# Radix-4 sums of four tiles as TensorE products, and a PSUM bank moved from the general ring to the first layer of the FFN, in a planned attention, FFT and FFN kernel

## The chip, the cores and the metric

The kernel runs on one core of one Trainium2 chip. The metric is the device time of one execution in microseconds; lower is better.

## The reference

Inputs: q, k, v of shape (8 batches, 8 heads, 576 positions, 64), float32, and the two weight matrices `w_ch1` (512 x 2048) and `w_ch2` (2048 x 512), which arrive as 8-byte floats. Output: (8, 576, 512), float32.

```python
scores = (1 / sqrt(64)) * q @ k.T            # causal window of 64 positions, else -1e9
attn   = softmax(scores) ; x = attn @ v      # x: (8, 576, 512), the heads side by side
mixed  = real(fft(fft(x, axis=1), axis=2))   # over the positions, then over the 512 columns
u      = x + mixed
un     = (u - mean(u)) / sqrt(var(u) + 1e-6) # over the 512 columns
out    = u + relu(un @ w_ch1) @ w_ch2
```

## The kernel before, in words

The 4608 rows are cut into 36 tiles T of 128 rows; nine tiles make a pair of batches. Each kind of work is written as a list of operations given to a planner (`Plan`), and nothing runs in the order in which it is written.

**Stages.** `attn_tile(T)` computes one tile of attention. Tiles 0 to 12 (`whole`) work in float32 with TensorE transposes; each fills nine PSUM banks: `pk` and `pq` (keys and queries turned), `psc` twice (scores), `pp` twice (probabilities turned), `pa` twice (attention times values), `py` (below). Tiles 13 to 35 split float32 into two float16 parts and turn them by DMA. In either form `normed` divides by the softmax's sum on VectorE (DVE), `radix4` makes four sums and differences of the 128-column quarters of x (two adds or subtracts of 128x256, two of 128x128, on DVE or GpSimd/POOL), and `flip_y` turns the four results onto the other axis by four TensorE transposes into a bank `py` (or by DMA in most tiles from 13 on). `fft(b)` does the two transforms of one batch when its tiles are there (after T = 4 and T = 8 of a pair), `norm_tile(T)` adds x and normalises, `ffn(c)` is the two-layer FFN of a chunk c of two tiles. For chunk 0 the FFN is in float32; for the other 17 each float32 product is three float16 products. The weights are converted from 8-byte floats by three DVE operations a piece (32 pieces, `conv`), and after chunk 0's use split into float16 parts (`weight_split`).

**FFN loop.** For each of 16 blocks f of 128 hidden columns `bank1`/`one` (line 1197) makes `ph` by 12 matmuls, ACT (line 1212) and DVE (line 1215) empty it into two float16 parts `hh`, and `second` (line 1178) multiplies these into `po`. Two blocks f share a bank of the ring `f1`; the bank is free when DVE's line 1215 of the second block is done.

**Rings.** Eight PSUM banks: `ps` 4 (all attention, FFT and normalisation stages but the first FFT's `pg`), `f1` 2, `f2` 2 (FFN output).

**The planner.** Each operation has an engine (or two, with `alt` and a margin), a duration, a latency, a priority (smaller is sooner) and the buffers it reads and writes. `order()` simulates the engines greedily from these durations and writes out one instruction order for each engine; the semaphores then hold that order on the chip, and every engine works its own queue strictly in order. All DMAs but the indirect ones are issued from SyncE's one queue (SP). Where the planned TensorE gap is over 0.8 us and no FFN has run yet, dummy matmuls (`warm`, line 1276) are written into it. `slack` is an allowance: an operation that can run on TensorE counts its inputs as ready later by `slack * LATE` of the engine that made them (DVE and ACT 0.5 us, POOL 0.7, DMA 1.0). It is 0.5 for tiles from T = 9 on and 0 for the first nine and for the FFN. A bank that comes free gets no such allowance.

```python
        "ps": 4, "f1": 2, "f2": 2,
                late = x.slack * self.LATE[o.eng] if "PE" in x.durs else 0.0
        op("POOL", 2.35, base + 7, radix4, [bx], [by], alt=("DVE", 1.2, LAZY_Y if T < 4 else lazy))
                nc.tensor.transpose(t["py"][:, j], t["y"][:, j], ident)
```

Of the kernel before, what the change touches and what calls it, by code (L numbers as in the profile page):

```python
# [12 lines left out]
F32 = mybir.dt.float32  # L13
# [28 lines left out]
Y_SOON = (4, 8)  # L42
LAZY, LAZY_FFT, LAZY_U = 0.4, 0.4, 0.5
LAZY_E, LAZY_Y = 0.3, 0.8
WARM = 0.8, 0.4
EARLY, LATER = 80, -20
PRO = 13
PITCH, FFT_AT, NORM_AT, FFT1 = 8.5, 13, 6, 0
SLACK = 0.5
PLAIN = 1  # L50
W_DMA, W_DMA_STEP, W_CONV, W_SQ, W_SPLIT, W_STEP = -40, 1.0, 20, 60, 60, 0.3
VS = 64.0
# [73 lines left out]
class Op:  # L126
    __slots__ = ("eng", "dur", "lat", "fn", "deps", "outs", "prio", "wait", "ready", "allocs", "bufs", "idx", "durs", "margin", "port", "slack")


class Plan:  # L130
# [13 lines left out]
    def __init__(self, rings, fifo):  # L144
        self.rings, self.fifo, self.ops, self.gaps = dict(rings), fifo, [], []
        self.slack = 0.0

    def op(self, eng, dur, prio, fn, reads=(), writes=(), lat=0.0, alt=(), holds=(), port=True):
# [4 lines left out]
        o.durs = {e: d + self.FIXED[e] for e, d in ([(eng, dur), alt[:2]] if alt else [(eng, dur)])}  # L153
        o.port, o.slack = port, self.slack
        o.margin = alt[2] if len(alt) > 2 else self.MARGIN
# [40 lines left out]
    def order(self):  # L196
# [23 lines left out]
        while len(res) < n:  # L220
# [77 lines left out]
def attn_fft_ffn_kernel(ctx: ExitStack, tc: tile.TileContext, q, k, v, w1, w2, gidx, dft_d, dft_s, mask, out):  # L298
# [112 lines left out]
    def attn_tile(T, base):  # L411
# [17 lines left out]
        bk, bq, bv = Buf("kq"), Buf("kq"), Bfl[3]  # L429
        op("DMA", 1.45, base - 8, lambda: load("kn", "kq", k), writes=[bk], lat=2.0)  # L430
        op("DMA", 1.45, base - 8, lambda: load("qn", "kq", q), writes=[bq], lat=2.0)
        if whole:
            op("DMA", 1.45, base - 6, lambda: load("vw", None, v), writes=[Bva[i]], lat=2.0)
        else:
            op("DMA", 1.45, base - 6, lambda: load("vn", None, v), writes=[bv], lat=2.0)

# [38 lines left out]
        else:  # L475
# [26 lines left out]
            op("POOL", 1.12, base + 0.1, k_lo, [bk], [bkp], alt=("DVE", 0.6, lazy))  # L502
            op("DMA", TURN, base + 0.2, k_turn, [bkp], [bkT], lat=2.0)
            op("ACT", 0.95, base + 0.5, lambda e: q_part(0, e), [bq], Bfl[4:6], alt=("DVE", 0.6, lazy))
            op("POOL", 2.1, base + 0.6, lambda e: q_part(1, e), [bq], Bfl[4:6], alt=("DVE", 1.13, lazy))
            for j in range(2):
                op("DMA", TURN, base + 0.7, lambda j=j: q_turn(j), Bfl[4:6], [Bq[i]], lat=2.8)
        if T == PRO and n > 0:

            def k_tail():  # L510
                src = kst32[:, (T - 1) % 3 * 512 : (T - 1) % 3 * 512 + 512].rearrange("p (a s) -> p a s", a=4)
                dst = kst16[:, before * 1024 : before * 1024 + 1024].rearrange("p (h s) -> p h s", h=H)
                for h in range(2):
# [9 lines left out]
            op("DVE", 1.6, base + 0.3, k_tail, [BkT[(T - 1) % 3]], [BkT[before], Buf("tail")])  # L523

# [32 lines left out]
        for jj in range(2):  # L557
# [73 lines left out]
            bpt[jj] = [bt, bt2]  # L631
            op("DMA", HTURN, base + 4.2 + jj, lambda g=p_turn: g(0), [bpp], [bt, bt2], lat=1.8)
            op("DMA", HTURN, base + 4.3 + jj, lambda g=p_turn: g(1), [bpp], [bt2], lat=1.8)

# [4 lines left out]
        for hf in range(2):  # L639
# [20 lines left out]

            def normed(hf=hf):
                pa = t["pa", hf]
                xv = xts[T].rearrange("p (h d) -> p h d", h=H)
                rc = sm.tile([P, 4, 1], F32, tag="rc", name=f"rc{T}_{hf}")
# [78 lines left out]
        def flip_y():  # L743
# [23 lines left out]
        if soon:  # L767
            op("PE", 0.44, base + 8, flip_y, [by, Bid], [bpy, *first])
        else:
            byp = Buf("up")  # L770
            op("ACT", 0.52, base + 7.5, y_hi, [by], [byp], alt=("DVE", 0.34, lazy))
            op("DVE", 0.6, base + 7.6, y_lo, [by], [byp])
            op("DMA", TURN, base + 7.7, y_turn, [byp], [bpy], lat=2.2)
        for a in keeps:
            op(*a, port=not soon)

    def fft(b, base):
# [120 lines left out]
        for cl in (1, 2, 0):  # L898
# [43 lines left out]
            op("PE", 0.67 if cl == 0 else 1.32, base + 5, sstage, [*(bg[gi] for _, gi in use), Bds], [bpz, bmp])  # L942
            op("ACT", 0.65, base + 5.1, odd, [bpz], [bmp])
            op("DVE", 1.2, base + 5.2, mix, [bpz], [bmp], port=False)
            if b == 0:
# [119 lines left out]
    def weight_piece(x, g, order):  # L1065
# [49 lines left out]
        op("DVE", 0.6, pr - 0.2, lambda: conv(2), bw, [bf])  # L1115
        op("ACT", 0.72, W_SQ + W_STEP * order, square, [bf], [bj, Bssq[x]])

# [127 lines left out]
    for T in range(NTT):  # L1245
        if T == PRO:
            to_parts()
        base = PITCH * T + (LATER if T > 4 else -EARLY)
        plan.slack = SLACK if T >= NT else 0.0
        attn_tile(T, base)  # L1250
        pb, n = divmod(T, NT)
# [5 lines left out]
        if T == 4:  # L1257
# [50 lines left out]
```

## Time and profile before

| | |
|---|---|
| median of three runs | 1010.4 us (1010.17 to 1551.11) |
| profiled execution | 1014.19 us, its span 1012.4 us |
| TensorE (PE) busy | 975.3 us, 96% of the span |
| VectorE (DVE) busy | 671.6 us, 66% |
| ACT busy | 417.3 us, 41% |
| POOL busy | 205.8 us, 20% |
| FFN's first product | 93.2 us after the start |

The span is what the trace shows; the execution lasts 1.8 us longer than it. Busy times are of one engine; an engine's waits are given with the engine and line that released it, and L1197 is line 1197 of the kernel above. The dummy matmuls count as busy.

### The profile page before, as it was taken

How to read it: one execution, taken by the hardware profiler on the slowest of the kernel's cores; microseconds unless marked ns; L12 is line 12 of the kernel's file. 1: busy time of each engine (PE TensorE's matmuls, PEld its weight loads, DVE VectorE, ACT ScalarE, POOL GpSimd, SP SyncE). 2: the span in 40 equal slices, each digit the busy share in tenths (PEclk: the TensorE clock that was granted, in tenths of full speed). 3: DMA queues.
4: the chain of work that ended last, by engine and by line, in shares of the span. 5: the costliest groups of instructions: out<-in, count | busy, mean ns of one | idle time of the engine just before them, and what ended most of it. 6: DMA issues, size and time to landing. Idle time of an engine off the chain costs nothing.

```text
span 1012.4 us, 22555 instructions
## 1 busy us (share of the span) xinstructions
PE 975.3 (96%) x8793; PEld 692.1 (68%) x8793; DVE 671.6 (66%) x1972; ACT 417.3 (41%) x1044; POOL 205.8 (20%) x211
## 2 busy tenths in 40 slices
PE   8888999999998999999999999999999999999998
PEld 6776768766675666666676667666676667666664
DVE  5889898887876758676776668666786555441121
ACT  6665667563544444344452345322454223211111
POOL 1001001133224403352132203141121300310000
PEclk9988999999999999999999999999999999999999
DMA  8978766533859896988768575857564411220000
GB/s 192 232 199 232 188 193 146 103 72 75 148 124 167 168 152 137 163 151 148 152 127 169 101 137 106 160 117 149 90 128 103 83 32 45 63 63 21 1 21 22
DMA packets 310955, 123.60 MB, mean 122 GB/s; under 512 B 292728, under 2 KB 292856, under 8 KB 310848
## 3 DMA queue, kind: packets, MB, share of 16 engines
q1 hardware_dynamic: 308128, 113.24, 55.3%
q0 software_dynamic: 2720, 8.92, 3.2%
q8 instruction: 69, 1.13, 0.5%
q14 instruction: 38, 0.31, 0.1%
HBM read 54.97 MB, written 14.17 MB: 68 GB/s over the span
## 4 chain that ended last, share of the span: by engine, by line
PE 73%; DMA 10%; DVE 9%; SPq 3%; ACT 2%; issue 2%; POOL 1%; DVEq 0%; ACTq 0%; POOLq 0%
PE ph L1197 31%; PE po L1178 28%; PE pa L657 3%; PE pg L878 2%; PE pz L910 2%; PE psc L568 2%; DMA uhl<-up 2%; DMA pt<-flex 2%; PE psc L575 2%; DMA kn<-in_k 1%; DMA mt<-md,gix 1%; DVE hh L1215 1%; SPq L626 1%; DMA qn<-in_q 1%; DVE y L691 1%
## 5 line engine op out<-in xcount | busy, mean ns | idle before, releaser
L1197 PE MATMUL ph<-uhl,w0s 128*128 128x256 f16 (+1 forms) x3384 | 427.5, 277 | 9.3 <-DVE hh L1215 8.6
L1178 PE MATMUL po<-w1s,hh 128*128 128x512 f16 (+1 forms) x1696 | 426.0, 387 | 0.2
L1197 PEld LDWEIGHTS <-w0s 128*128 128x128 f16 x3264 | 318.5, 98 | 96.8 <-issue 14.3
L1215 DVE SCALAR_TENSOR_TENSOR hh<-ph,hh 128x256 f16<-128x256 f32 x272 | 114.6, 422 | 223.8 <-ACT hh L1212 212.2
L1212 ACT ACTIVATE hh<-ph 128x256 f16<-128x256 f32 x272 | 104.1, 383 | 375.5 <-PE ph L1197 264.5
L1178 PEld LDWEIGHTS <-hh 128*128 128x128 f16 x1632 | 155.9, 98 | 139.5 <-issue 1.0
L595 ACT ACTIVATE pr<-pr,nm 128x128 f32<-128x128 f32 x288 | 91.3, 393 | 16.3 <-DVE nm L587 16.3
L587 DVE CUSTOM_DVE_ANT_0 pr<-psc,mskb 128x128 f32<-128x128 f32 x288 | 65.7, 286 | 15.9 <-PE psc L568 11.8
L1012 POOL TENSOR_TENSOR rs<-mv,mhalf 128x1 f32<-128x1 f32 x36 | 21.6, 599 | 181.0 <-DVE mv L1008 160.2
L1035 POOL TENSOR_TENSOR up<-un,up 128x512 f16<-128x512 f32 x33 | 39.0, 1183 | 70.4 <-ACT up L403 63.6
L620 POOL TENSOR_TENSOR flex<-pr,flex 128x512 f16<-128x512 f32 x25 | 30.0, 1202 | 109.5 <-ACT flex L403 90.7
L657 PE MATMUL pa<-va,pt 128*64 128x65 f16 (+1 forms) x760 | 41.5, 207 | 5.7 <-DMA pt<-flex 5.1
L988 POOL DMA_INDIRECT mt<-md,gix x34 | 35.9, 1057 | 52.0 <-DMA md<-mp 46.4
L657 PE MATMUL pa<-ve,pt 128*64 128x65 f16 (+1 forms) x760 | 42.0, 208 | 0.1
L484 POOL TENSOR_TENSOR flex<-kn,flex 128x512 f16<-128x512 f32 x19 | 22.7, 1197 | 83.6 <-ACT flex L403 82.1
L403 ACT CAST flex<-pr 128x512 f16<-128x512 f32 x38 | 23.5, 620 | 27.7 <-DMA pt<-flex 25.5
L669 DVE TENSOR_TENSOR xu<-pa,rc 128x256 f32<-128x256 f32 x72 | 30.6, 425 | 2.9 <-DMA out<-xu 0.3
L568 PE MATMUL psc<-kst,qbd 128*128 128x128 f32 x208 | 29.8, 293 | 2.5 <-ACT qbd L403 1.2
L691 DVE TENSOR_TENSOR y<-xu 128x256 f32<-128x256 f32 x70 | 30.2, 472 | 0.6
L657 PEld LDWEIGHTS <-pt 128*64 128x64 f16 x1104 | 20.8, 112 | 14.0 <-issue 7.2
L568 PEld LDWEIGHTS psc<-kst,qbd 128*128 128x128 f32 x208 | 26.9, 203 | 4.5 <-issue 1.9
L910 PE MATMUL pz<-g,ds__75 97*96 97x257 f16 (+3 forms) x240 | 29.2, 273 | 0.5 <-DVE g L888 0.5
(156 smaller groups left out, 1115.1 us busy)
## 6 DMA issues: line engine op xcount, KB each, us to landing
wd<-in_moe_w_ch SPq DMA_DIRECT2D x20, 512.0 KB
out<-xu SPq DMA_DIRECT2D x36, 256.0 KB
ve<-va SPq DMA_DIRECT2D x67, 130.0 KB
kn<-in_k SPq DMA_DIRECT2D x32, 256.0 KB
qn<-in_q SPq DMA_DIRECT2D x32, 256.0 KB
flex<-in_moe_w_ch SPq DMA_DIRECT2D x12, 512.0 KB
flex<-in_v SPq DMA_DIRECT2D x20, 256.0 KB
md<-mp SPq DMA_DIRECT2D x24, 192.0 KB
```

The source lines that it names most:

```text
L568: nc.tensor.matmul(p_[:, hp], qw, keys(hp, jj), start=True, stop=True)
L587: nc.vector.tensor_tensor_reduce(out=t["pr", jj][:, hp], in0=t["ps", jj][:, hp], in1=mskb[:, m : m + P], scale=-0.125, scalar=3.0e38, op0= ...
L595: nc.scalar.activation(pr, pr, AF.Exp, bias=t["nm", jj][:, hp : hp + 1], scale=-1.0)
L657: nc.tensor.matmul(pa[64 * jj : 64 * jj + 64, hh], pt[:, sl], v_, start=(x == 0), stop=(x == len(mm) - 1))
L691: eng.tensor_tensor(out=o, in0=p0, in1=p1, op=al)
L910: nc.tensor.matmul(pz[:M, c0:c1], ds_[:NJ, a, c[0] : c[0] + c[1]], t["g", gi][:, b_, c0:c1], start=(x == 0), stop=(x == len(mm) - 1),)
L988: nc.gpsimd.indirect_dma_start(out=mts[T], out_offset=None, in_=mds[pb][0 : HR if n < 4 else 2 * HR], in_offset=bass.IndirectOffsetOnAxis( ...
L1035: eng.tensor_tensor(out=t["up"][:, 1], in0=t["un"], in1=t["up"][:, 0], op=ALU.subtract)
L1178: nc.tensor.matmul(t["po"][i], l_, r_, start=(f == 0 and x == 0), stop=(f == NKF - 1 and x == len(mm) - 1))
L1197: nc.tensor.matmul(ph, l_, r_, start=(x == 0), stop=(x == len(mm) - 1))
L1212: nc.scalar.activation(t["hh", f][:, 0], ph, AF.Relu)
L1215: nc.vector.scalar_tensor_tensor(out=hh[:, 1], in0=ph, scalar=0.0, in1=hh[:, 0], op0=ALU.max, op1=ALU.subtract)
```

## The change

1. For T in `Y_SUMS` = (1, 2, 3, 4) the operation `radix4` is gone. `flip_y` reads x itself and makes each of the four turned sums by accumulating float32 matmuls of the quarters against the identity or its negative (`minus`, a new constant made on POOL): 4 + 4 + 2 + 2 = 12 matmuls in place of 4 transposes.
2. The ring `ps` has 3 banks in place of 4, `f1` 3 in place of 2.
3. `normed` is cut in two: the reciprocal stays on DVE, and the multiplication may go to ACT as four scaled copies of 128x64.
4. The planner gets a second allowance, `wary`: operations that cannot run on TensorE count inputs from another engine as late by 0.6 `LATE` in all stages but the conversion of the weights and the FFN of chunks 1 to 17; `slack` for TensorE becomes 0.
5. Planned durations and DMA latencies are set anew, and so are priorities (tiles from T = 5 on 30 us later, weight conversion 20, squares 50, split 10 later, the weights' DMAs 10 later, the second FFT of the first pair 10 later, since it has 20 less of its own) and margins for the choice of engine.

```diff
-LAZY, LAZY_FFT, LAZY_U = 0.4, 0.4, 0.5
+LAZY, LAZY_FFT, LAZY_U = 0.1, 0.8, 0.2
-EARLY, LATER = 80, -20
+EARLY, LATER = 80, 10
-PITCH, FFT_AT, NORM_AT, FFT1 = 8.5, 13, 6, 0
-SLACK = 0.5
+PITCH, FFT_AT, NORM_AT, FFT1 = 8.5, 13, 9, -20
+SLACK = 0.0
+SLACK_V = 0.6
+WARY = 0
+LAZY_N = 0.0
+Y_SUMS = (1, 2, 3, 4)
-W_DMA, W_DMA_STEP, W_CONV, W_SQ, W_SPLIT, W_STEP = -40, 1.0, 20, 60, 60, 0.3
+W_DMA, W_DMA_STEP, W_CONV, W_SQ, W_SPLIT, W_STEP = -30, 1.0, 40, 110, 70, 0.3
...
-                late = x.slack * self.LATE[o.eng] if "PE" in x.durs else 0.0
+                late = self.LATE[o.eng] * (x.slack if "PE" in x.durs else 0.0 if o.eng in x.durs else x.wary)
...
-        "ps": 4, "f1": 2, "f2": 2,
+        "ps": 3, "f1": 3, "f2": 2,
...
-            op("DMA", HTURN, base + 4.2 + jj, lambda g=p_turn: g(0), [bpp], [bt, bt2], lat=1.8)
+            op("DMA", HTURN, base + 4.2 + jj, lambda g=p_turn: g(0), [bpp], [bt, bt2], lat=2.4)
...
+            def normed(eng, hf=hf):
+                pa, rc = t["pa", hf], t["rc", hf]
+                xv = xts[T].rearrange("p (h d) -> p h d", h=H)[:, 4 * hf : 4 * hf + 4]
+                if eng is nc.scalar:
+                    for hh in range(4):
+                        nc.scalar.mul(xv[:, hh], pa[:, hh, 0:64], rc[:, hh])
+                else:
+                    eng.tensor_tensor(out=xv, in0=pa[:, :, 0:64], in1=rc.to_broadcast([P, 4, 64]), op=ALU.mult)
...
-            op("DVE", 0.75, base + 6.2 + 0.5 * hf, normed, [bpa], [bx], port=False)
+            brc = Buf()
+            op("DVE", 0.26, base + 6.2 + 0.5 * hf, recip, [bpa], [brc], port=False)
+            op("DVE", 0.32, base + 6.25 + 0.5 * hf, normed, [bpa, brc], [bx], alt=("ACT", 0.95, LAZY_N), port=False)
...
-        op("POOL", 2.35, base + 7, radix4, [bx], [by], alt=("DVE", 1.2, LAZY_Y if T < 4 else lazy))
+        summed = T in Y_SUMS
+        if not summed:
+            op("POOL", 3.2, base + 7, radix4, [bx], [by], alt=("DVE", 1.2, LAZY_Y if T < 4 else lazy))
...
-            for j in range(4):
-                nc.tensor.transpose(t["py"][:, j], t["y"][:, j], ident)
+            for j, terms in enumerate(((0, 1, 2, 3), (0, 5, 2, 7), (0, 6), (1, 7))):
+                if summed:
+                    for x, m in enumerate(terms):
+                        quarter = xts[T][:, P * (m % 4) : P * (m % 4) + P]
+                        nc.tensor.matmul(
+                            t["py"][:, j], quarter, ident if m < 4 else minus, start=(x == 0), stop=(x == len(terms) - 1)
+                        )
+                else:
+                    nc.tensor.transpose(t["py"][:, j], t["y"][:, j], ident)
...
-            op("PE", 0.44, base + 8, flip_y, [by, Bid], [bpy, *first])
+            op("PE", 2.85 if summed else 0.44, base + 8, flip_y, [bx if summed else by, Bid], [bpy, *first])
...
+        plan.wary = SLACK_V if T >= WARY else 0.0
```

Of the other latencies, loads of q, k and v go from 2.0 to 2.5 us, the turning of keys from 2.0 to 2.2, of queries from 2.8 to 3.0, of y from 2.2 to 3.0; `radix4` on POOL is planned at 3.2 us for 2.35.

## Rows read from the trace of the kernel before

**Rows 1.** The page's first two parts: busy time of each engine, and PE's busy share in 40 equal slices of the span, 25.3 us each (tenths).

```profile
PE 975.3 (96%) x8793; PEld 692.1 (68%) x8793; DVE 671.6 (66%) x1972; ACT 417.3 (41%) x1044; POOL 205.8 (20%) x211
PE   8888999999998999999999999999999999999998
```

**Rows 2.** Busy time of each engine in seven stretches of the span (columns: stretch, its length, then each engine's busy us with its instructions, granted clock, DMA share, GB/s).

```profile
0.00:16.00 16.00, 12.63 (x110) 10.34 (x111) 5.35 (x31) 7.93 (x18) 3.33 (x13) 1.00 0.87 178
16.00:47.50 31.50, 27.63 (x292) 23.37 (x290) 27.05 (x118) 22.73 (x60) 1.87 (x1) 0.95 0.92 223
47.50:72.00 24.50, 20.41 (x199) 17.99 (x199) 21.61 (x54) 14.27 (x38) 0.69 (x2) 0.86 0.82 211
72.00:93.20 21.20, 15.40 (x149) 12.86 (x147) 19.43 (x61) 12.81 (x34) 2.82 (x3) 0.84 0.82 232
93.20:200.00 106.80, 106.80 (x749) 79.81 (x748) 94.76 (x270) 68.16 (x167) 12.79 (x13) 1.00 0.67 163
200.00:810.00 610.00, 594.69 (x5852) 413.09 (x5850) 434.61 (x1288) 255.19 (x634) 168.97 (x164) 1.00 0.69 130
810.00:1012.40 202.40, 197.75 (x1454) 134.69 (x1452) 68.78 (x157) 36.21 (x95) 15.34 (x16) 1.00 0.13 34
```

**Rows 3.** The same stretches for the dummy matmuls of line 1276 alone (PE busy, PEld busy, clock, DMA share, GB/s): the stretch from 16 us, and the answer's sum over all seven.

```profile
16.00:47.50 31.50, 2.38 (x16) 1.57 (x16) 0.95 0.92 223
...
sum 1012.40, PE 19.45 PEld 13.83; mean PE 2.78 PEld 1.98
```

**Rows 4.** What PE waited for between 200 and 810 us (total us, times, longest).

```profile
PE ph L1197 <- DVE hh L1215: 8.0, 12, 1.7
PE pa L657 <- DMA pt<-flex: 5.1, 4, 3.2
PE py L750 <- DVE y L691: 0.9, 1, 0.9
```

**Rows 5.** The longest of PE's waits for line 1215 and another of over a microsecond: timelines of DVE and of PE (start us, us, what; in brackets the idle time before and who ended it).

```profile
545.05 0.43 DVE L407 CAST flex<-kn 128x512 f16<-128x512 f32 x1 [2.70 <-DMA kn<-in_k]
545.39 0.42 DVE L1215 SCALAR_TENSOR_TENSOR hh<-ph,hh 128x256 f16<-128x256 f32 x1
...
540.13 1.47 PE L1197 MATMUL ph<-uhl,w0s 128*128 128x256 f16 x12
541.44 1.46 PE L1178 MATMUL po<-w1s,hh 128*128 128x512 f16 x6
542.74 1.47 PE L1197 MATMUL ph<-uhl,w0s 128*128 128x256 f16 x12
545.86 2.30 PE L1197 MATMUL ph<-uhl,w0s 128*128 128x256 f16 x18 [1.65 <-DVE hh L1215]
...
685.62 0.69 DVE L1000 TENSOR_TENSOR xu<-xu,mt 128x511 f32<-128x511 f32 x1 [1.73 <-DMA mt<-md,gix]
...
687.90 1.47 PE L1197 MATMUL ph<-uhl,w0s 128*128 128x256 f16 x12 [1.39 <-DVE hh L1215]
```

**Rows 6.** What PE waited for before the FFN begins, 0 to 93.2 us (the four longest).

```profile
PE pp L606 <- ACT pr L595: 3.7, 1, 3.7
PE pk L464 <- DMA kn<-in_k: 3.1, 2, 2.5
PE pk L464 <- ACT qbd L403: 1.7, 1, 1.7
PE pq L464 <- DMA qn<-in_q: 1.5, 2, 0.9
```

**Rows 7.** From the chain that ended last, cut to 0 to 105 us (start us, us, what): float32 products of 128 columns at full and at half clock, float32 transposes, a DMA of weights, and the FFN's first product.

```profile
30.67 2.95 PE psc L568 x16
...
36.72 0.89 PE psc L568 x8
...
74.28 4.86 DMA flex<-in_moe_w_ch
...
93.21 5.18 PE ph L1197 x24
98.40 0.44 PE py L750 x4
```

**Rows 8.** DVE's timeline: the radix-4 sums of tiles 1 and 4, with what follows.

```profile
25.95 0.76 DVE L691 TENSOR_TENSOR y<-xu 128x256 f32<-128x256 f32 x2
26.63 0.61 DVE L691 TENSOR_TENSOR y<-y 128x128 f32<-128x128 f32 x2
...
46.31 0.76 DVE L691 TENSOR_TENSOR y<-xu 128x256 f32<-128x256 f32 x2
...
47.52 0.96 DVE L794 TENSOR_TENSOR yT<-yT 128x772 f32<-128x772 f32 x1
```

**Rows 9.** Groups by line over the whole span (count, busy us, mean ns): the normalising multiplication on DVE, and ACT reading PSUM in its smallest form.

```profile
L669 DVE TENSOR_TENSOR xu<-pa,rc 128x256 f32<-128x256 f32 x72 | 30.6, 425 | 2.9 <-DMA out<-xu 0.3
L927 ACT COPY mp<-pz 96x2 f32<-96x2 f32 (+1 forms) x24 | 4.1, 173 | 0.0
```

**Rows 10.** Filling and emptying of `ps` banks: the first row of PE's timeline that fills one after 16.2 us, and the DVE row that empties the last one counted (34 fillings, begun between 16.25 and 44.2 us).

```profile
16.25 0.60 PE L464 MATMUL pk<-ident,kn 128*128 128x128 f32 x4
...
45.85 0.42 DVE L669 TENSOR_TENSOR xu<-pa,rc 128x256 f32<-128x256 f32 x1
```

More of the change, by code (lines that the diff above doesn't have):

```diff
@@ L126 @@
 class Op:
-    __slots__ = ("eng", "dur", "lat", "fn", "deps", "outs", "prio", "wait", "ready", "allocs", "bufs", "idx", "durs", "margin", "port", "slack")
+    __slots__ = ("eng", "dur", "lat", "fn", "deps", "outs", "prio", "wait", "ready", "allocs", "bufs", "idx", "durs", "margin", "port", "slack", "wary")
 class Plan:
@@ L145, in __init__ @@
         self.rings, self.fifo, self.ops, self.gaps = dict(rings), fifo, [], []
-        self.slack = 0.0
+        self.slack = self.wary = 0.0
     def op(self, eng, dur, prio, fn, reads=(), writes=(), lat=0.0, alt=(), holds=(), port=True):
@@ L153, in op @@
         o.durs = {e: d + self.FIXED[e] for e, d in ([(eng, dur), alt[:2]] if alt else [(eng, dur)])}
-        o.port, o.slack = port, self.slack
+        o.port, o.slack, o.wary = port, self.slack, self.wary
         o.margin = alt[2] if len(alt) > 2 else self.MARGIN
@@ L323, in attn_fft_ffn_kernel @@
     ident = cp.tile([P, P], F32, name="ident")
+    minus = cp.tile([P, P], F32, name="minus")
     mhalf = cp.tile([P, 1], F32, name="mhalf")
@@ L362, in attn_fft_ffn_kernel @@
     op("POOL", 0.3, -500, lambda: make_identity(nc, ident), writes=[Bid])
+    op("POOL", 0.4, -480, lambda: nc.gpsimd.tensor_scalar(out=minus, in0=ident, scalar1=-1.0, scalar2=None, op0=ALU.mult), [Bid], [Bid])
     op("POOL", 0.1, -499, lambda: nc.gpsimd.memset(mhalf, -0.5), writes=[Bmh])
@@ L429, in attn_tile @@
         bk, bq, bv = Buf("kq"), Buf("kq"), Bfl[3]
-        op("DMA", 1.45, base - 8, lambda: load("kn", "kq", k), writes=[bk], lat=2.0)
-        op("DMA", 1.45, base - 8, lambda: load("qn", "kq", q), writes=[bq], lat=2.0)
+        op("DMA", 1.45, base - 8, lambda: load("kn", "kq", k), writes=[bk], lat=2.5)
+        op("DMA", 1.45, base - 8, lambda: load("qn", "kq", q), writes=[bq], lat=2.5)
         if whole:
-            op("DMA", 1.45, base - 6, lambda: load("vw", None, v), writes=[Bva[i]], lat=2.0)
+            op("DMA", 1.45, base - 6, lambda: load("vw", None, v), writes=[Bva[i]], lat=2.5)
         else:
-            op("DMA", 1.45, base - 6, lambda: load("vn", None, v), writes=[bv], lat=2.0)
+            op("DMA", 1.45, base - 6, lambda: load("vn", None, v), writes=[bv], lat=2.5)
         bkT = BkT[T % 3]
@@ L502, in attn_tile @@
             op("POOL", 1.12, base + 0.1, k_lo, [bk], [bkp], alt=("DVE", 0.6, lazy))
-            op("DMA", TURN, base + 0.2, k_turn, [bkp], [bkT], lat=2.0)
+            op("DMA", TURN, base + 0.2, k_turn, [bkp], [bkT], lat=2.2)
             op("ACT", 0.95, base + 0.5, lambda e: q_part(0, e), [bq], Bfl[4:6], alt=("DVE", 0.6, lazy))
@@ L506, in attn_tile @@
             for j in range(2):
-                op("DMA", TURN, base + 0.7, lambda j=j: q_turn(j), Bfl[4:6], [Bq[i]], lat=2.8)
+                op("DMA", TURN, base + 0.7, lambda j=j: q_turn(j), Bfl[4:6], [Bq[i]], lat=3.0)
         if T == PRO and n > 0:
@@ L521, in k_tail @@
                     nc.vector.tensor_tensor(out=lo, in0=old, in1=hi, op=ALU.subtract)
-            op("DVE", 1.6, base + 0.3, k_tail, [BkT[(T - 1) % 3]], [BkT[before], Buf("tail")])
+            op("DVE", 3.0, base + 0.3, k_tail, [BkT[(T - 1) % 3]], [BkT[before], Buf("tail")])
         def v_part(z):
@@ L631, in attn_tile @@
             bpt[jj] = [bt, bt2]
-            op("DMA", HTURN, base + 4.2 + jj, lambda g=p_turn: g(0), [bpp], [bt, bt2], lat=1.8)
-            op("DMA", HTURN, base + 4.3 + jj, lambda g=p_turn: g(1), [bpp], [bt2], lat=1.8)
+            op("DMA", HTURN, base + 4.2 + jj, lambda g=p_turn: g(0), [bpp], [bt, bt2], lat=2.4)
+            op("DMA", HTURN, base + 4.3 + jj, lambda g=p_turn: g(1), [bpp], [bt2], lat=2.4)
         bx, by = Buf("xu"), Buf("y")
@@ L659, in av, with recip @@
                             )
-            def normed(hf=hf):
+            def recip(hf=hf):
                 pa = t["pa", hf]
-                xv = xts[T].rearrange("p (h d) -> p h d", h=H)
-                rc = sm.tile([P, 4, 1], F32, tag="rc", name=f"rc{T}_{hf}")
+                rc = t["rc", hf] = sm.tile([P, 4, 1], F32, tag="rc", name=f"rc{T}_{hf}")
                 nc.vector.tensor_scalar(
@@ L772, in attn_tile @@
             op("DVE", 0.6, base + 7.6, y_lo, [by], [byp])
-            op("DMA", TURN, base + 7.7, y_turn, [byp], [bpy], lat=2.2)
+            op("DMA", TURN, base + 7.7, y_turn, [byp], [bpy], lat=3.0)
         for a in keeps:
@@ L942, in fft @@
             op("PE", 0.67 if cl == 0 else 1.32, base + 5, sstage, [*(bg[gi] for _, gi in use), Bds], [bpz, bmp])
-            op("ACT", 0.65, base + 5.1, odd, [bpz], [bmp])
-            op("DVE", 1.2, base + 5.2, mix, [bpz], [bmp], port=False)
+            op("ACT", 0.39, base + 5.1, odd, [bpz], [bmp])
+            op("DVE", 1.03, base + 5.2, mix, [bpz], [bmp], port=False)
             if b == 0:
@@ L1115, in weight_piece @@
         op("DVE", 0.6, pr - 0.2, lambda: conv(2), bw, [bf])
-        op("ACT", 0.72, W_SQ + W_STEP * order, square, [bf], [bj, Bssq[x]])
+        op("ACT", 0.53, W_SQ + W_STEP * order, square, [bf], [bj, Bssq[x]])
     def weight_scale(x, prio):
@@ L1263, in attn_fft_ffn_kernel @@
                 weight_split(x, g, W_SPLIT + W_STEP * i)
-    plan.slack = 0.0
+    plan.slack = plan.wary = 0.0
     for c in range(PLAIN, NCH):
```

3 lines of the change are left out of this document (removed).

## Prediction

> **What bounds the kernel now.** I read the busy shares first. TensorE is busy 96% of the span, VectorE 66%, and the slices show PE at nine tenths or more from the fourth on but for one [rows 1]. So a microsecond counts only where PE stands still, runs dummies or runs at half clock. The stretches say where that is [rows 2]. Before the first FFN product, at 93.2 us, PE is busy 12.63 + 27.63 + 20.41 + 15.40 = 76.1 us, of which up to 19.45 are dummies [rows 3]: some 36 of the 93.2 us are idle or dummy, and the granted clock means 0.84 to 0.95 in three of the four stretches. From 93.2 to 200 PE has no idle time. From 200 to 810 it is idle 610 - 594.69 = 15.3 us, and after that 4.7. DVE is the other full engine of the start: 27.05 of 31.50 us from 16 to 47.5, when tiles 1 to 4 are made.
>
> What ended PE's waits in the long middle is in the list of waits [rows 4]: 8.0 us in 12 waits of the first FFN layer for DVE's line 1215 (the emptying of an `f1` bank), 5.1 us in 4 waits for the DMA that turns probabilities, 0.9 for a radix-4 sum. The timelines show what the 8.0 us are [rows 5]. At 542.3 us DVE has nothing left but an instruction that waits for keys still in flight; the DMA lands at 545.05, and only behind that cast does line 1215 run, at 545.39; PE, out of banks, had been idle for 1.65 us. At 685.62 it is a gathered `mt` in place of keys. DVE isn't slow there; its order puts a DMA's landing ahead of the bank's release, and PE has one other bank to live on.
>
> **The change part by part.** The sum is made against the profiled execution (1014.2 us, 3.8 above the median of the runs shown), and its differences are put on the median.
>
> *The third `f1` bank.* A bank holds two blocks of the FFN. A block is 12 matmuls of the first layer and six of the second, which begin 1.31 and 1.30 us before the next ones [rows 5]. So one more bank lets PE work on for up to 5 us when DVE is stuck, and the longest such wait is 1.65 us [rows 5]. All of the 8.0 us [rows 4] are within reach. I take -7.5 and leave 0.5, as a planner that sees three free banks will again plan up to the third. Bounds: -8.0, and 0 if it does so everywhere (a rival below).
>
> *The third bank taken from `ps`.* No row of PE's waits from 200 us on names the emptying of a `ps` bank [rows 4]. There a tile is made every 22 us or so, and fills four of them. I charge +1, bounds 0 and +3 (the 0.9 us of the one `py` wait, three times). In the start it is otherwise: nine fillings to a tile. Pairing each filling's first write with its last read in the timelines gives 34 fillings in 28 us (the first and the last are in [rows 10]), held 1.96 us on average, 66.7 bank-us: 2.4 banks of four are taken. This goes into the next term and into a rival.
>
> *The sums as products.* Removed: four DVE instructions a tile for tiles 1 to 4, 25.95 to 27.24, so 1.3 us a tile [rows 8], 5.2 us of DVE's 27.05 in that stretch. Added: 12 float32 products for 4 transposes. Eight records of `psc`, that is four products, take 0.89 us, four transposes 0.44 [rows 7]; so 12 x 0.222 = 2.67 against 0.44, +2.23 us a tile and +8.9 us in all at full clock (at half clock, where 16 records took 2.95 us, two thirds more). Per tile the chain from x to `py` goes from 1.3 + 0.44 to 2.67 us: longer by 0.9, but without DVE's queue in the middle. Is there room on PE? In 16 to 47.5 it is busy 27.63, 2.38 of it dummies; 25.25 + 8.9 = 34.2 us for a stretch of 31.5 [rows 2, 3]. So PE, not DVE, would set this stretch, at +2.6 us. If instead DVE stays the limit, it is -5.2. If later PE work (tiles 5 and 6) is pushed behind 93.2, where PE is full, all of the 8.9 is paid. I take 0 for the start: the two limits nearly cancel, the tile-4 sum just ahead of the FFT's first fold [rows 8] is a real relief, and the 36 us of idle and dummy time can take 8.9 us of products. Bounds -5.2 and +8.9.
>
> A rule speaks against this part. The Trainium skill (Perfetto Trace Analysis, Transposes) asks that a logical transpose be done as a transpose and not as a standard matmul, and its page TensorE: Matmul & The Clock Gate (Terms) calls transpose mode four times faster for float32. The rows agree on the direction but say twice, 0.222 against 0.111 us; by the page's factor, as an estimate, the 12 products would take 5.3 us and the four tiles +19 us instead of +8.9. The rows decide.
>
> *The later allowances and latencies.* The turning of probabilities was planned to land 1.8 us after its issue plus 0.5 of slack for PE, 2.3; now 2.4, and 0.6 x 0.7 = 0.42 are allowed ahead of it where POOL made the part, so 2.8. Half a microsecond more takes 0.5 off each of the four waits of 5.1 us [rows 4]: -2.0. Bounds: -5.1, and 0. Against it, PE's own allowance goes to zero, so a late ACT or DVE is met unpadded; before 93.2 us, where it was zero already, the longest such waits are 3.7 (about when the chain runs through a weights' DMA of 4.86 us) and 1.7 us [rows 6, 7]. In the middle PE has FFN work to interleave, so +1, bounds 0 and +5. What is queued behind an unpadded wait is all of PE's order.
>
> *The split of `normed`.* On DVE nothing is added, as the same three instructions run. Where ACT takes the multiplication, DVE loses 0.425 us and ACT gets four small copies of at least 0.173 each [rows 9], 0.7 us or more; ACT is busy 22.73 of 31.5 us in the tightest stretch [rows 2]. Nothing of PE's path: 0.
>
> *The moved priorities.* They shift queues in the start: the weights' DMAs and conversion and all of tiles 5 and up on SP, DVE, ACT. Only waits for loads bound it: 3.1 + 1.5 us [rows 6], either way. I take 0, as the weights keep their place ahead of tile 5's loads (-30 to +1 against 44, before -40 to -9 against 14), and the FFT of tile 4 its place ahead of all conversion. The later squares and splits lie on ACT and DVE after 93.2 us, beside a full PE.
>
> Sum: -7.5 + 1 + 0 - 2.0 + 1 + 0 + 0 = -7.5. Profiled execution 1006.7, median **1002.9**, say 1003.
>
> **The rivals.**
> *The start shortens too.* Tile 4's sums are out of DVE's queue right before the fold that starts the FFT, and the FFN begins at the end of that chain [rows 7, 8]. If DVE's 5.2 us pass through to 93.2 and the order takes 3 of the waits for loads, 1003 - 8 = 995. For it: DVE at 86% in that stretch. Against: PE's 34.2 us.
>
> *The start is starved of `ps` banks, and the kernel is slower.* The place is 16 to 47.5 us. With `py` held 2.2 us longer in four tiles the 34 fillings need 75.6 bank-us; three banks in 28 us offer 84. Packed at 90% this costs nothing. It decides as soon as the mean hold rises from 2.22 to above 2.47 us. If three banks are used no better than four are today (60%), 75.6 / 1.8 = 42 us in place of 28: +14 and 1017. For it: in order, a late evacuation stops everything behind it on PE. Against: the holds are long because banks were plenty.
>
> *The bank does nothing.* FFN operations have neither slack nor `wary`, so the planner may place line 1215 as tightly against three banks as against two, and a DMA ahead of it on DVE stops PE as before; the other small terms cancel: 1010. Against it: the wait is for real lateness of a DMA, which the plan, with its longer latencies, now foresees better.
>
> **How the numbers follow.** Chances: forecast 0.45 (998 to 1008), shorter start 0.20 (988 to 998), starved start 0.13 (1010 to 1025), idle bank 0.17 (1008 to 1013), else 0.05. The range of 8 in 10 takes the forecast and the idle bank whole, and most of the shorter and the starved start: 988 to 1017. Two per cent, about what a measurement of this kernel can tell from no change, is 20 us: under 990.2 needs the best ends together (-8.0 - 5.1 - 5.2 - 4.6 is -22.9), 0.11; over 1030.6 the starved start at its worst, 0.04.
>
> **What would show it.** Right: the waits of line 1197 for line 1215 under 1 us in the middle; from 200 to 810 PE idle some 5 us less; line 1197 first at 93 +- 3 us; 48 `py` products more, busy near 100% in 16 to 47.5 with fewer dummies and a clock nearer 1.0. Wrong: the first FFN product well before 90 us (shorter start) or after 100 with PE waits for ACT or DVE emptying `pk`, `pq`, `psc` (starved), or waits for line 1215 that are still 8 us (idle bank). What I cannot see, an order that the planner finds and no term here holds, would make it wrong most easily, since one changed priority rewrites every queue.

## The result, and the profile after

| | before | after |
|---|---|---|
| median of the runs | 1010.3 us (1009.91 to 1551.11) | 1023.7 us (1014.12 to 1024.72) |
| profiled execution, its span | 1014.19 us, 1012.4 us | 1014.12 us, 1012.0 us |

The ratio on record is 1.0094, interval 1.0065 to 1.0123; it leaves out one slow execution of before, of 1551.11 us. So the change is 0.9% slower (1.3% by the medians of the table), where 0.7% faster was forecast, and its median lies 6.7 us above the range. The profile of after is of its shortest execution; a second profile, of the first run below, is of one of 1021.3 us, and both are used.

The page's busy times, and TensorE's (PE's) slices, of after:

```profile
PE 977.5 (97%) x8844; PEld 691.9 (68%) x8844; DVE 696.1 (69%) x2005; ACT 411.7 (41%) x1053; POOL 168.7 (17%) x175
PE   8987999999999999999999999999999999999998
```

The seven stretches of [rows 2] for after (stretch, length, busy us of each engine, granted clock, DMA share, GB/s):

```profile
0.00:16.00 16.00, 12.73 (x105) 10.41 (x107) 6.18 (x29) 7.58 (x18) 3.81 (x14) 1.00 0.85 199
16.00:47.50 31.50, 29.56 (x312) 26.13 (x308) 23.20 (x105) 22.55 (x61) 0.00 (x0) 1.00 0.97 241
47.50:72.00 24.50, 20.41 (x239) 17.67 (x237) 23.21 (x63) 18.38 (x49) 1.93 (x3) 1.00 0.83 214
72.00:93.20 21.20, 15.37 (x164) 12.41 (x166) 19.18 (x74) 14.63 (x45) 1.65 (x2) 1.00 0.80 225
93.20:200.00 106.80, 103.99 (x720) 76.07 (x716) 94.07 (x248) 69.02 (x163) 12.64 (x11) 1.00 0.64 157
200.00:810.00 610.00, 597.72 (x5873) 414.64 (x5871) 459.91 (x1335) 242.09 (x627) 138.47 (x133) 1.00 0.68 129
810.00:1012.40 202.40, 197.67 (x1453) 134.55 (x1451) 70.33 (x160) 37.46 (x96) 10.18 (x12) 0.99 0.15 35
```

In the start the clock is 1.00 throughout, where [rows 2] has 0.95, 0.86 and 0.84; DVE is down by 3.9 us and PE up by 1.9 in 16 to 47.5. From 93.2 to 200 PE now has 2.8 us idle, since the first FFN product comes at 99.5 us in place of 93.2. What it waited for from 200 to 810 (total us, times, longest):

```profile
PE ph L1220 <- DVE hh L1238: 8.4, 11, 1.7
PE py L773 <- DVE y L704: 2.4, 3, 1.0
PE ph L1220 <- DMA uhl<-up: 0.6, 1, 0.6
PE pa L663 <- DMA pt<-flex: 0.5, 1, 0.5
```

Line 1220 is 1197 of before, 1238 is 1215. The 5.1 us for turned probabilities of [rows 4] are nearly gone. The 8.0 us for DVE's emptying, which a third bank was to take away, are 8.4.

**A ledger.** Busy time hides half clock and dummies, so I also add up the columns of every recorded matmul but the dummies at full clock (12 x 256 columns are 1.28 us; [rows 5] has 1.30 to 1.31; a float32 product of 128 columns 0.213, where 0.222 was read; products on 64 columns of weights start in pairs 3 to 4 ns apart and are counted at half) and call the rest of the time lost. The work is 898.8 us before and 907.3 after: the products are 8.5 us. Lost, us:

| | to 93.2 | 93.2 to 330 | 330 to 810 | from 810 | at half clock |
|---|---|---|---|---|---|
| before | 50.1 | 18.7 | 35.8 | 9.1 | 20.6 |
| after, its profile | 40.6 | 16.9 | 38.4 | 8.8 | 2.0 |
| after, second profile | 40.6 | 17.1 | 45.0 | 9.2 | 8.3 |

Of the half clock, the 2.0 us of after's profile and 1.5 of the second one's 8.3 lie behind PE's last matmul and cost nothing. So up to 93.2 us the start pays the products in full (-9.5 against +8.5), and the middle, where the gain was to be, loses 2.6 us more than before in one execution and 9.2 in the other. These 9.2 are 3.1 of waits for DVE's emptying (10.6 for 7.5 in this stretch), 2.4 of waits for radix-4 sums, 3.4 lost at half clock (experiment 1) and 0.3 of other things.

### The profile page after: what moved, and what is told of

It reads as the page before. It is cut to its first block, busy times and chain, and to the rows that moved or that the text cites. A ratio compares the mean times of both kernels' runs of the same rounds, so it can differ in the third digit from the quotient of the medians.

```text
span 1012.0 us, 22672 instructions
## 1 busy us (share of the span) xinstructions
PE 977.5 (97%) x8844; PEld 691.9 (68%) x8844; DVE 696.1 (69%) x2005; ACT 411.7 (41%) x1053; POOL 168.7 (17%) x175
## 4 chain that ended last, share of the span: by engine, by line
PE 76%; DVE 14%; DMA 4%; ACT 2%; issue 2%; SPq 1%; POOL 0%; DVEq 0%; ACTq 0%; POOLq 0%
PE ph L1220 33%; PE po L1201 30%; PE pa L663 2%; PE pz L933 2%; PE pg L901 2%; PE psc L581 2%; PE psc L574 2%; DVE y L704 2%; DVE hh L1238 1%; DMA wd<-in_moe_w_ch 1%; DVE pr L593 1%; DMA flex<-in_moe_w_ch 1%; PE pp L612 1%; DMA uhl<-up 1%; PE py L773 1%
## 5 line engine op out<-in xcount | busy, mean ns | idle before, releaser
L626 POOL TENSOR_TENSOR flex<-pr,flex 128x512 f16<-128x512 f32 x22 | 26.6, 1211 | 109.3 <-ACT flex L409 64.1
L490 POOL TENSOR_TENSOR flex<-kn,flex 128x512 f16<-128x512 f32 x20 | 25.2, 1262 | 100.6 <-ACT flex L409 75.1
L663 PE MATMUL pa<-ve,pt 128*64 128x65 f16 (+1 forms) x760 | 39.7, 204 | 0.9 <-ACT pt L409 0.5
L663 PE MATMUL pa<-va,pt 128*64 128x65 f16 (+1 forms) x760 | 39.3, 204 | 0.7 <-DMA pt<-flex 0.5
L501 POOL TENSOR_TENSOR flex<-qn,flex 128x1024 f16<-128x1024 f32 x11 | 24.5, 2223 | 36.8 <-ACT flex L409 19.9
L581 PEld LDWEIGHTS <-qbd 128*64 128x64 f16 x736 | 21.7, 109 | 11.8 <-issue 10.9
L933 PEld LDWEIGHTS <-ds__76 97*96 97x96 f16 (+1 forms) x240 | 26.5, 123 | 4.3 <-issue 3.1
L682 DVE TENSOR_TENSOR xu<-pa,rc 128x256 f32<-128x256 f32 x65 | 27.2, 423 | 2.0
```

The costliest lines, as they stand in the source:

```text
L581: nc.tensor.matmul(p_[64 * x : 64 * x + 64, hp], qbd[i][:, jj, h, 64 * z : 64 * z + 64], keys(h, jj), start=(z == 0), stop=(z == 1),)
L663: nc.tensor.matmul(pa[64 * jj : 64 * jj + 64, hh], pt[:, sl], v_, start=(x == 0), stop=(x == len(mm) - 1))
L933: nc.tensor.matmul(pz[:M, c0:c1], ds_[:NJ, a, c[0] : c[0] + c[1]], t["g", gi][:, b_, c0:c1], start=(x == 0), stop=(x == len(mm) - 1),)
```

## The experiments

Times are medians; each ratio is to runs of before on the same chip, with a 95% interval. Before's medians on the three chips used are 1013.0 us (experiments 1 and 2), 1011.8 (the first kernels of 3 and 7, all of 5 and 6) and 1012.3 (the rest). An edit moves the lines below it: lines 1220 and 1238 of after are 1218 and 1236 or 1234 in some kernels, and 1197 and 1215 of before are 1195 and 1211.

**1. The changed kernel again, and a lower threshold for dummies.** After unchanged, and after with

```diff
-WARM = 0.8, 0.4
+WARM = 0.35, 0.2
```

> The changed kernel once more, unaltered. Theory (the clock): its two times, 1014 and 1023 to 1025 us, are the same order with TensorE at full clock through the start (granted clock 0.999) and with some 8 to 14 us of half clock (0.993 to 0.996); an execution at 0.993 to 0.996 takes 1022 to 1025, one at 0.999 takes 1014, and a trace of the first shows half clock before 100 us. Rival: the time is lost elsewhere (a DMA that lands late in the middle), and the clock doesn't go with the time.

> The changed kernel's order, with dummy matmuls in planned TensorE gaps from 0.35 us on in place of 0.8 (that is the only edit). Theory (the clock): the dummies keep the clock up in the start, so executions come at 0.998 or more and at 1013 to 1016 us each. Rival (not the clock): times still lie at 1014 and at 1023 to 1025, or the dummies delay the products behind them and all are at 1020 or more.

Measured: 1020.7 us, ratio 1.0088 (1.0058 to 1.0119), and with more dummies 1021.8, 1.0106 (1.0064 to 1.0147), at a mean clock of 0.999 in the profile. The slowdown repeats, and a nearly full clock doesn't remove it. Both clock theories fall: executions at 0.998 took 1020.3 and 1021.2 us, and the second profile has no half clock before 100 us. PE's waits in that second profile of after from 200 us on (the same columns), and then two of its windows (as the stretches above):

```profile
PE ph L1220 <- DVE hh L1238: 11.2, 12, 2.7
PE py L773 <- DVE y L704: 2.4, 3, 1.0
PE pa L663 <- DMA pt<-flex: 1.7, 2, 1.4
```

```profile
423.00:427.00 4.00, 1.32 (x11) 0.84 (x10) 3.90 (x15) 1.28 (x4) 2.06 (x3) 1.00 0.51 96
427.00:431.00 4.00, 4.00 (x18) 2.05 (x16) 3.90 (x7) 0.89 (x2) 0.68 (x1) 0.57 0.37 98
```

PE stood still for 2.7 of the four microseconds up to 427, for line 1238, and the next four ran at 0.57 of the clock. The other wait of over 2 us, up to 525.6, is followed by the same. So each of these two waits cost its own length and part of a stretch at 1.2 GHz: 6.8 us at half clock behind the two, 3.4 us lost. Not every such wait does: with more dummies PE waited 2.1 us up to 657.7, and the next 4.2 us ran at a granted clock of 1.00.

**2. Is the third bank spent by the planner?** The plan of two `f1` banks, once with two banks on the chip and once with three, so that the third is pure slack:

```diff
-        "ps": 3, "f1": 3, "f2": 2,
+        "ps": 3, "f1": 2, "f2": 2,
...
-        return ps.tile(list(shape), F32, tag=tag, name=name, bufs=RINGS[tag])
+        return ps.tile(list(shape), F32, tag=tag, name=name, bufs=3 if tag == "f1" else RINGS[tag])
```

(the second edit in the second kernel alone).

> The changed kernel with ps 3 and f1 2, so one of the eight banks lies unused; the plan is made for these. Both theories: waits of the first FFN layer for DVE's emptying of 8 us or more between 200 and 810 us, time 1015 to 1030. It is the reference for the next kernel.

> The same plan and the same order of instructions as the run before, but the program has three f1 banks while the plan counted on two; the third bank is real slack. Theory (the planner spends the bank it knows of): the waits for the emptying fall under 2 us and the time is 5 to 10 us below the run before. Rival (a third bank can't help, as DVE stands longer than a bank covers): the same waits within 2 us, the same time within 3 us.

Measured: 1019.1 us, 1.0073 (1.0042 to 1.0104), and 1018.2, 1.0056 (1.0029 to 1.0082). PE's waits for DVE's emptying from 200 us on, with two banks:

```profile
PE ph L1220 <- DVE hh L1238: 3.9, 7, 1.4
```

With the third bank as slack that nobody planned on, PE still waits for DVE:

```profile
PE ph L1220 <- DVE hh L1238: 5.5, 9, 1.4
PE py L773 <- DVE y L704: 3.9, 2, 3.5
PE pa L663 <- DMA pt<-flex: 3.5, 3, 2.1
```

A free bank doesn't shorten these waits, so they aren't waits for a bank, and the theory that the planner spends it falls. The two-bank kernel has less than half of the 8 us that were expected, and yet is within 1.6 us of after: these waits alone don't set the time of an order. The Trainium skill (Perfetto Trace Analysis, Optimization Strategy) reads a gap that repeats as a possible lack of PSUM, in buffer count or tile size; here the count was tried and gave 0.9 us, inside the spread of the runs.

**3. The wait is inside a bank.** The kernel's list of instructions says what the first matmul of each block waits for, and the trace how long. In after all eleven waits for line 1238 between 200 and 810 us come at the second block of a pair, and are for the emptying of the *first* block in the same bank; in the second profile all eleven, too. In before ten of the twelve do (5.5 us). The other two (2.5 us, with the longest, up to 545.86) come at the first block of a pair and are for a whole bank, the only kind that a further bank can shorten; in after none of that kind is left. The planner's model has no dependency inside a bank. The list has such a wait at 87 of the 136 second blocks of chunks 1 to 17 of after, where the plan writes DVE's emptying of block 2k ahead of block 2k+1; these can't begin before 2k has been emptied, however many banks are free. (In most other pairs the plan lets block 2k+1 go first.) It is a semaphore of the program that holds PE back; whether the chip would need it was not tried. Tested in after's own instruction order, by giving each block a bank of its own and leaving half of it empty:

```diff
-                if f % 2 == 0:
-                    t["ph2", f] = bank("f1", f"ph{c}_{f}", (P, 2, CH))
-                t["ph", f] = t["ph2", f - f % 2][:, f % 2]
+                t["ph", f] = bank("f1", f"ph{c}_{f}", (P, 2, CH))[:, 0]
```

> The changed kernel in its own order; the one edit is where the first layer's results lie: each block f has one of the three f1 banks to itself, in place of two blocks sharing one. Theory (the wait is inside a bank: the second block's first matmul waits until DVE has emptied the first block of the same bank, so rings of any depth leave it): all waits of the first layer for DVE's emptying between 200 and 810 us fall from 8 to under 2 us, and the time falls by 5 to 9 us against the changed kernel, to about 1012 to 1015. Rival (DVE stands longer than PE can be kept going by banks): waits of 5 us or more stay, time within 3 us of the changed kernel's 1020.7.

Measured: 1019.5 us, 1.0064 (1.0045 to 1.0084). From 200 to 810 no wait for DVE's emptying is left, and PE is busy 602.4 us of 610 in place of 597.7. But the gain goes back in the last chunk (waits from 810 us on, and PE's timeline):

```profile
PE ph L1220 <- DVE hh L1236: 8.4, 9, 0.9
```

```profile
975.72 1.47 PE L1220 MATMUL ph<-uhl,w0s 128*128 128x256 f16 x12 [0.93 <-DVE hh L1236]
977.02 1.46 PE L1201 MATMUL po<-w1s,hh 128*128 128x512 f16 x6
979.41 1.47 PE L1220 MATMUL ph<-uhl,w0s 128*128 128x256 f16 x12 [0.93 <-DVE hh L1236]
```

Nine equal waits: this order was written for six blocks in flight, and with one to a bank there are three. So own banks for chunks 0 to 16 and pairs in the last alone, in the same order again:

```diff
-                if f % 2 == 0:
+                own = c < 17
+                if own or f % 2 == 0:
...
-                t["ph", f] = t["ph2", f - f % 2][:, f % 2]
+                t["ph", f] = t["ph2", f][:, 0] if own else t["ph2", f - f % 2][:, f % 2]
```

> The changed kernel in its own order, each block of the first layer with a bank of its own in chunks 0 to 16; the last chunk keeps two blocks to a bank. (With all chunks changed the last one alone lost 8.4 us in 9 waits from 974 us on, since its order was planned for six blocks in flight.) Theory (inside the bank): the middle's gain is kept and the end's loss gone, so 1010 to 1013 us, 8 us below the changed kernel's 1020.7. Rival (the order, not the bank, sets the middle): 1017 or more.

Measured: 1009.5 us (1005.9 to 1012.4), 0.997 (0.9953 to 0.9988): 11.2 us under after (1020.7) with the same order, work and ring. PE's waits from 200 us on, all of them:

```profile
PE pa L663 <- DMA pt<-flex: 2.0, 3, 0.8
PE pz L933 <- DVE g L911: 1.6, 2, 1.0
PE pg L901 <- DVE nm L593: 1.3, 1, 1.3
PE py L773 <- DVE y L704: 0.7, 2, 0.4
PE ph L1220 <- DMA uhl<-up: 0.5, 1, 0.5
PE psc L581 <- DMA qbd<-flex: 0.3, 1, 0.3
```

Not one is for line 1238, and the time lost from 330 to 810 is 31.9 us against 45.0. The Trainium skill (Perfetto Trace Analysis, Matmuls) asks that independent matmul groups rotate through different PSUM banks so that one's evacuation overlaps the next's matmuls; these 11.2 us are what that rule is worth here.

**4. What makes DVE late.** In [rows 5] it was a DMA's landing ahead in DVE's queue. In after it is mostly POOL. Timelines of DVE, POOL and PE at the longest wait of the profile of after (start us, us, what):

```profile
622.42 1.03 DVE L869 TENSOR_TENSOR hs<-h,hs 128x388 f16<-128x388 f32 x2
623.37 3.65 DVE L704 TENSOR_TENSOR y<-xu 128x256 f32<-128x256 f32 x2
626.94 0.60 DVE L704 TENSOR_TENSOR y<-y 128x128 f32<-128x128 f32 x2
627.46 0.42 DVE L1238 SCALAR_TENSOR_TENSOR hh<-ph,hh 128x256 f16<-128x256 f32 x1
...
623.05 1.41 POOL L490 TENSOR_TENSOR flex<-kn,flex 128x512 f16<-128x512 f32 x1 [5.71 <-ACT flex L409]
624.43 2.30 POOL L501 TENSOR_TENSOR flex<-qn,flex 128x1024 f16<-128x1024 f32 x1
...
624.73 1.46 PE L1201 MATMUL po<-w1s,hh 128*128 128x512 f16 x6
627.93 1.47 PE L1220 MATMUL ph<-uhl,w0s 128*128 128x256 f16 x12 [1.74 <-DVE hh L1238]
```

Two radix-4 sums, 0.42 us each as a rule, take 3.65 us together and end 0.3 us after POOL's second subtraction. Against the median of their kind, 33 DVE instructions of after (40 of before) are over 0.15 us too long, 32.9 us in all (27.8), and every one overlaps a POOL instruction. The Trainium skill (SBUF — State Buffer, SBUF: two separate sides) says that the two engines share one pair of ports, which a POOL instruction, or a DVE one of some kinds (those with two inputs in SBUF among them), locks for its whole length; the ends 0.3 us apart fit that. Not every DVE instruction is held up: 233 of after lie wholly within a POOL instruction and none of them is too long by as much. DMA landings still count: the longest wait of the second profile, 2.7 us up to 426.2, has none of this ahead of it, but DVE idle for a gathered `mt`. The instruction in the second profile, then in the first:

```profile
422.06 0.68 DVE L1023 TENSOR_TENSOR xu<-xu,mt 64x511 f32<-64x511 f32 x1 [3.32 <-DMA mt<-md,gix]
418.49 0.68 DVE L1023 TENSOR_TENSOR xu<-xu,mt 64x511 f32<-64x511 f32 x1 [0.49 <-DMA mt<-md,gix]
```

In the kernel with own banks in chunks 0 to 16, 32 DVE instructions are 31.8 us too long. The place of the 1.74 us wait there, DVE, then PE:

```profile
620.34 3.65 DVE L704 TENSOR_TENSOR y<-xu 128x256 f32<-128x256 f32 x2
...
623.00 1.47 PE L1220 MATMUL ph<-uhl,w0s 128*128 128x256 f16 x12
625.74 0.71 PE L901 MATMUL pg<-dd,fs 128*128 128x65 f16 x12 [1.27 <-DVE nm L593]
```

DVE is just as late, PE runs its next block all the same, and 1.27 of the 1.74 us come back at a later step that needs DVE. The lateness is not cured but met with more work in hand; PE's waits between 330 and 810 fall from 15.2 us (second profile of after) to 6.4.

**5. Are the products hidden?** One product in place of each sum, 4 of 12 a tile, in after's order:

```diff
-                    for x, m in enumerate(terms):
+                    for x, m in enumerate(terms[:1]):
...
-                            t["py"][:, j], quarter, ident if m < 4 else minus, start=(x == 0), stop=(x == len(terms) - 1)
+                            t["py"][:, j], quarter, ident if m < 4 else minus, start=(x == 0), stop=True
```

> The changed kernel in its own order; each turned sum of tiles 1 to 4 is made of its first term alone, so 4 of the 12 products of a tile are left and 32 x 0.222 = 7.1 us of TensorE work are gone (the sums of these tiles are left out, and the output with them). Theory (the start is a chain through TensorE, so the products are paid): the first FFN product comes 5 to 7 us sooner, at 92.5 to 95 us, and the time falls by 5 to 8 us. Rival (idle time hides them, as the prediction had it): first FFN product at 98 to 100 us as before, time within 2 us.

Measured: 1019.3 us, 1.0060 (1.0037 to 1.0083), 1.5 us under after (2.8 by the ratios) for 6.8 us less work (900.5 us by the ledger). The time lost up to 93.2 us rises from 40.6 to 48.2, and the first FFN product comes at 102.0. So the products stand for the most part in time that PE would otherwise lose: 1.5 to 2.8 of the 6.8 us are paid.

**6. What a new order costs by itself.** Before, with a spacing of priorities changed by 1% and nothing else:

```diff
-PITCH, FFT_AT, NORM_AT, FFT1 = 8.5, 13, 6, 0
+PITCH, FFT_AT, NORM_AT, FFT1 = 8.6, 13, 6, 0
```

> The kernel before with one priority pitch changed from 8.5 to 8.6, nothing else: the same work in another order. Theory (a new order alone moves the time by as much as the whole change did): it differs from the kernel before by 3 to 12 us, either way. Rival (the order hardly matters): within 2 us.

Measured: 1021.6 us, 1.0091 (1.0059 to 1.0123): as slow as after. PE's waits from 200 us on:

```profile
PE ph L1197 <- DVE hh L1215: 10.8, 12, 2.0
PE ph L1197 <- DMA uhl<-up: 6.1, 1, 6.1
PE pa L657 <- DMA pt<-flex: 1.9, 5, 0.5
```

Lost from 330 to 810: 47.8 us against 35.8. So a 0.9% loss needs no cause in the change's own parts; another order of the same work does it.

**7. Own banks planned.** Before's plan made anew with each block holding a bank (`f1` 2, `ps` 4 as before), and the same with the 1% edit of experiment 6:

```diff
-            bph, bh = Buf(), Buf("hh")
-            if f % 2 == 0:
-                bpair, bfirst = Buf("f1"), Buf()
+            bph, bh = Buf("f1"), Buf("hh")
...
-                if f % 2 == 0:
-                    t["ph2", f] = bank("f1", f"ph{c}_{f}", (P, 2, CH))
-                t["ph", f] = t["ph2", f - f % 2][:, f % 2]
+                t["ph", f] = bank("f1", f"ph{c}_{f}", (P, 2, CH))[:, 0]
...
-            op("PE", 1.73 if plain else 1.31, 1e6 + 32 * c + 2 * f, bank1, [Bu[c], *bws, bfirst], [bph] if f % 2 else [bph, bfirst], holds=[bpair])
+            op("PE", 1.73 if plain else 1.31, 1e6 + 32 * c + 2 * f, bank1, [Bu[c], *bws], [bph])
```

(and no `holds=[bpair]` at the two steps that empty it).

> The kernel before, planned anew with each block of the FFN's first layer in a bank of its own (two f1 banks, ps 4 as before). Theory (inside the bank): the waits of 8.0 us in the middle fall under 3 us; the time is 3 to 8 us below the kernel before, if the new order costs nothing. Rival (two banks with one block each leave PE no room): waits of the first layer for DVE of 8 us or more, time the same or longer.

> The kernel before with a bank for each block (1000.5 us) and the priority pitch 8.6 for 8.5, the change that cost 9.8 us where blocks shared banks. Theory (the spread between orders came from the waits inside the banks): within 4 us of 1000.5, waits of the first layer for DVE under 3 us. Rival (the spread is of orders as such): 6 us or more away.

Measured: **1000.5 us** (999.6 to 1001.3), 0.9885 (0.9848 to 0.9921), the fastest of all; and 1005.5, 0.9930 (0.9908 to 0.9951). The 1% edit costs 5.0 us here, 9.8 with pairs: in this one pair of orders half of the loss is gone with own banks. That it went through the shared banks isn't shown: in experiment 6 the waits for DVE's emptying from 200 us on are only 2.2 us above before's 8.6, while a wait of 6.1 us for a chunk's input is new, and that one is 1.8 us here. Before with own banks, PE's waits from 200 us on (the longest), and its stretch from 200 to 810:

```profile
PE pa L657 <- DMA pt<-flex: 1.5, 2, 1.3
PE pg L878 <- DVE hs L846: 1.4, 1, 1.4
PE ph L1195 <- DVE hh L1211: 1.2, 1, 1.2
```

```profile
200.00:810.00 610.00, 603.85 (x5988) 420.96 (x5987) 450.73 (x1315) 255.38 (x641) 161.60 (x153) 1.00 0.71 131
```

PE is idle 6.2 us of these 610, before 15.3 [rows 2].

**8. The whole change on own banks.** After planned anew in the same way (`f1` 3, `ps` 3), with the products and, by `Y_SUMS = ()`, without.

> The changed kernel with each block in a bank of its own and planned so (three f1 banks, ps 3). Theory (products hidden in the start, waits gone): PE's lost time up to 330 us as in the changed kernel, the waits for DVE's emptying under 2 us all through, 998 to 1006 us. Rival (three banks of ps cost the middle, or the new order draws badly): 1010 or more with waits for other banks or DMAs.

> As the run of the changed kernel with a bank of its own for each block, but without the products: tiles 1 to 4 make their radix-4 sums on DVE or POOL again. Theory (the start's idle time pays the products): the same time within 3 us, PE's useful work 8.5 us less and its lost time before 93 us 8 to 10 us more. Rival (products shorten the start): 4 us or more slower than with them; rival (products are paid): 6 us or more faster.

Measured: 1014.2 us, 1.0010 (0.9992 to 1.0028), and 1009.7, 0.9970 (0.9949 to 0.9991). PE's waits from 200 us on, the longest of the one with products and of the one without:

```profile
PE ph L1218 <- DMA uhl<-up: 10.3, 2, 8.3
```

```profile
PE ph L1218 <- DMA uhl<-up: 5.7, 1, 5.7
```

Both wait for a chunk's input, by 4.6 us more with products, as much as the medians differ by. The first kernel missed its 998 to 1006, as the rival had it, and the difference lies between the theory (3) and the rival (6) of the second. The lost time to 93.2 us is 41.1 with products and 49.9 without, against 8.5 us of work: up to there the start takes the products at no cost here too, and buys nothing with them. But the first FFN product comes at 101.0 us for 93.2, and from 93.2 to 330 us 16.0 are lost for 13.2; how much of the 4.6 us is the products and how much the other order isn't shown. Neither comes near 1000.5 us: that kernel has none of this change's other parts.

## Why the prediction was wrong, step by step

- **The third bank, -7.5: the step that failed.** "So one more bank lets PE work on for up to 5 us" and "All of the 8.0 us are within reach" took every wait for one for a free bank, from the words of the ring. The reading of the wait up to 545.86 was right: that one, and one more, were for a bank, 2.5 us together, and after has none left. The other ten of before, 5.5 us, were for the other half of the same bank, which no further bank shortens; there are eleven of them in after. Measured: 8.4 us left of 8.0 in the profile, 11.0 in the second one. The rival "the bank does nothing" had the size of this term, but its mechanism, a planner that spends the bank, falls with experiment 2. The kernel before could have told: its list of instructions has the waits at second halves.
- **The bank taken from `ps`, +1.** No wait from 200 us on names one of its banks' emptying by itself, and the start wasn't starved: lost time to 93.2 us fell by 9.5. The starved-start rival did not occur.
- **The products, 0.** Nearly right: +8.5 us of work (I had 8.9), paid by time lost before, so -1.0 to 93.2; in one and the same order (experiment 5) 1.5 to 2.8 of 6.8 us are paid. The 48 products are there (96 records), and they took the place reckoned: PE is 29.56 of 31.50 us busy from 16 to 47.5, 1.58 of it dummies for 2.38 [rows 3], the clock at 1.00. The first FFN product at 99.5 lies outside 93 +- 3, and PE is idle for 2.8 us from 93.2 to 200 (2.9 in the second profile), where before is never; but FFN chunk 4 begins at 331 us in before and in both profiles of after. The shorter start didn't come.
- **Allowances and latencies, -2.0 and +1.** The wait for turned probabilities fell by 4.6 us (3.4 in the second profile), inside the bounds but twice the value; the unpadded one for a radix-4 sum grew by 1.5.
- **`normed`, 0.** ACT took seven of 72 half tiles, as 28 copies of 0.314 us; one of them held PE up, for 0.4 us, before 93.2.
- **The priorities, 0.** Experiment 6 is the price of such a term: +9.8 us for a neutral 1%. "One changed priority rewrites every queue" stood in the text and not in the range, whose upper end came from the start alone. This is the second thing that failed: the redraw was put at nothing, with no number behind that.
- **A reading.** The slices of [rows 1] show nine tenths from the fifth on but for two, not from the fourth on but for one; nothing hangs on it.

From the forecast for a profile (1006.7 us) to the second one (1021.3) it is 14.6 us: 10.5 are the third bank (+3.0 in place of -7.5), 1.7 half clock (3.4 behind the two long waits, less 1.7 in before behind its wait of 3.2 us for probabilities), +0.5 the sums, -1.4 the probabilities, -1.0 the bank from `ps`, -1.0 the start and +2.9 PE's idle time from 93.2 to 200; 2.4 are left.

What stays open: why executions of one and the same order lie between 1014 and 1025 us. More dummies didn't narrow it to the short ones. The two profiles, 7.2 us apart, differ mainly in two waits for line 1238 (up to 426 and 526) that are 2.7 and 0.7 us longer, and in the 3.4 us lost at half clock behind them; the first goes back to a DMA's landing (experiment 4), but why that came late isn't shown. Nor is it shown which part of the change makes its order lose more than before's, or why own banks planned for after lose 10.3 us to a chunk's input, where before's plan doesn't.

## What to carry to other kernels

Before giving a ring another bank, look which block waits: where it is the second of two groups in one bank, more banks do nothing, and one group to a bank does (11.2 us in the same order; 6.5 to 16 with a plan made for it, which is a new order too). A forecast for a change that makes the planner write a new order needs a term for the redraw; measure it once with a neutral change of one priority, and make no less of it than of the edits. Work that is moved into a stretch with idle time is nearly free there, but a gain needs the stretch's end to move.

## What the runs showed of the hardware

Beside a POOL elementwise instruction a DVE one of 0.42 us took up to 2.3 us, and ended 0.3 us after POOL's; 33 DVE instructions so held up were 32.9 us too long in all, of DVE's 696, while 233 others within a POOL instruction were not. And in the second profile of after PE's waits of 2.7 and 2.2 us were each followed by 3.4 us at 1.2 GHz, so that they cost more than they show. Length alone doesn't decide: in the last kernel of experiment 7 a wait of 2.3 us up to 613.7 was followed by a granted clock of 1.00.
